# Larger weight loads, two columns through all weights first, columns 2 and 3 transposed by DMA: a gated unit beside a spectral filter

## The chip, the cores and the metric

The kernel runs on one core of a Trainium2 chip. The metric is the device time of one execution in microseconds (us), as a median of several executions. All traces shown are of executions in the fast state, with a granted TensorE clock of 0.998 or more. One execution of the kernel before was slow (183.37, clock 0.991); it counts in the median of its batch, 180.18 (180.00 without it), and not in the ratios. Ratios are the mean time of one kernel's fast runs over that of the other's in the same rounds, so they are not quite the ratio of the medians quoted beside them. An effect of 1 us is 0.56%. The medians of the kernel before lie up to 0.5% apart from batch to batch (179.32 to 180.18), so a kernel is compared only with the kernel before of its own batch.

## The reference, cut to what matters

```python
x  = A_x                                   # 2048 rows of 512, bf16
xn = layernorm(x)                          # over the 512
X  = rfft2(xn) * (w_r + 1j*w_i)            # spectral filter
A  = irfft2(X)
g  = xn @ w_gate;  u = xn @ w_up           # 512 -> 1792
B  = (gelu(g) * u) @ w_down                # 1792 -> 512
return x + A + B
```

The 2048 rows are held as 16 "columns" of 128 rows. The 1792 hidden features are 14 "weight columns" of 128. The gated unit is the large part of the matmul work; the spectral transform is done by matrix products in between.

## The kernel before: the parts that matter

The kernel makes its own plan: each operation has an engine, a guessed duration, dependencies and a priority, and a small planner puts them in an order per engine. In the traces each engine takes its instructions in that order; semaphores only make it wait.

```python
plan = _Plan({"S": 4, "G": 2, "U": 2, "ge": 3, ...})   # buffers: two PSUM banks for u
...
load_x(0, 1); d_ident = load_ct("ident", ...); load_x(1, 1)
load_w(0, 2, ("SP", "ACT")); load_x(2, 2); load_w(2, 4); load_w(4, 6)
load_x(4, 4); load_w(6, 10); load_x(8, 4); load_w(10, 14)
...
for c in range(4):                 # columns 0 to 3: transposed by TensorE
    ...; pe_transpose(c, -28 + 3 * c)
for c0, n, due in ((4, 2, 14), (6, 2, 16), (8, 4, 24), (12, 4, 32)):
    layernorm(c0, n, due)
    for c in range(c0, c0 + n): dma_transpose(c, due)
...
# glu(c0, n, f0, nf): n columns, nf weight columns: g_ps, u_ps on TensorE,
# ge = gelu(g_ps) on ScalarE, hT = u_ps * ge on VectorE, which frees the PSUM bank of u_ps
FIRST = [(0, 1, 0, 4), (1, 1, 0, 4), (0, 2, 4, 2), (2, 2, 0, 2), (2, 2, 2, 2), (2, 2, 4, 2)]
for c, n, f, nf in FIRST + [(0, 4, f, 1) for f in range(6, NFC)]: glu(c, n, f, nf)
```

The names in the traces: `x_t` input, `st` its statistics, `xn` normalized, `tp` transposes on TensorE, `xnT` transposed activations, `g_ps`/`u_ps` gate and up products, `hT` their product, `xf` a fold of `xn` for the transform, `bp` the first transform product, `RF_t` its table, `TW` the filter table, fetched by gathers on GpSimd. PE is TensorE, PEld its weight loads, DVE is VectorE, ACT ScalarE, POOL GpSimd; SPq and ACTq are the DMA issues of SyncE and ScalarE. PSUM is the memory that TensorE writes its products to.

## Time and profile before

| | before |
|---|---|
| time, median (first three runs) | 179.28 us |
| span of the trace | 177.6 us |
| first gated matmul | 6.89 us |
| end of the last product | 174.86 us |

Matmuls are pipelined, so the busy share hides small holes. I found gaps by the pitch: a group of n matmuls that starts at t is through its issue at t + n times the price of its width (0.056, 0.109, 0.2155 us for 128, 256, 512 columns), and the gap is what lies between that and the start of the next group.

### The profile page before, as it was taken

How to read it: one execution, taken by the hardware profiler on the slowest of the kernel's cores; microseconds unless marked ns; L12 is line 12 of the kernel's file. 1: busy time of each engine (PE TensorE's matmuls, PEld its weight loads, DVE VectorE, ACT ScalarE, POOL GpSimd, SP SyncE). 2: the span in 40 equal slices, each digit the busy share in tenths (PEclk: the TensorE clock that was granted, in tenths of full speed). 3: DMA queues.
4: the chain of work that ended last, by engine and by line, in shares of the span. 5: the costliest groups of instructions: out<-in, count | busy, mean ns of one | idle time of the engine just before them, and what ended most of it. 6: DMA issues, size and time to landing. Idle time of an engine off the chain costs nothing.

```text
span 177.6 us, 3041 instructions
## 1 busy us (share of the span) xinstructions
PE 173.4 (98%) x1100; PEld 92.9 (52%) x1100; DVE 118.1 (66%) x266; ACT 87.4 (49%) x158; POOL 18.6 (10%) x33
## 2 busy tenths in 40 slices
PE   6999999999999999999999999999999999999993
PEld 2598545545554544554555455554445444544463
DVE  1869999999537995889999885336442541632522
ACT  3162437456789737999998855453111211211100
POOL 3212138743200000000000000000000000000000
PEclk9999999999999999999999999999999999999999
DMA  5999487999297001302211121100222221322212
GB/s 144 311 355 359 86 270 84 223 296 193 52 347 255 2 0 29 93 2 59 61 48 37 37 59 37 27 0 0 84 68 66 83 89 59 92 80 69 74 45 59
DMA packets 23182, 19.24 MB, mean 108 GB/s; under 512 B 8512, under 2 KB 21824, under 8 KB 23168
## 3 DMA queue, kind: packets, MB, share of 16 engines
q1 hardware_dynamic: 22176, 17.57, 35.0%
q0 software_dynamic: 320, 1.19, 3.1%
q10 hardware_dynamic: 672, 0.30, 0.6%
q8 instruction: 8, 0.13, 0.3%
q14 instruction: 6, 0.05, 0.1%
HBM read 13.28 MB, written 2.10 MB: 87 GB/s over the span
## 4 chain that ended last, share of the span: by engine, by line
PE 91%; ACT 3%; DVE 3%; issue 1%; POOL 0%; DVEq 0%; POOLq 0%
PE u_ps L502 25%; PE g_ps L502 25%; PE warm L380 3%; ACT E L652 2%; PE yp L818 2%; PE bp L581 2%; PE gp L767 2%; PE yp__2078 L872 2%; PE yp__1994 L872 2%; PE yp__1967 L872 2%; PE yp__1936 L872 2%; PE yp__1909 L872 2%; PE yp__1820 L872 2%; PE yp__1793 L872 2%; PE yp__1762 L872 2%; PE yp__1735 L872 2%
## 5 line engine op out<-in xcount | busy, mean ns | idle before, releaser
L502 PE MATMUL g_ps<-xnT,Wg_sb 128*128 128x512 bf16 (+2 forms) x264 | 58.1, 347 | 0.0
L502 PE MATMUL u_ps<-xnT,Wu_sb 128*128 128x512 bf16 (+2 forms) x264 | 57.9, 347 | 0.0
L527 DVE TENSOR_TENSOR hT<-u_ps,ge 128x512 bf16<-128x512 f32 x56 | 38.4, 685 | 17.5 <-PE u_ps L502 14.4
L519 ACT ACTIVATE ge<-g_ps 128x512 bf16<-128x512 f32 x56 | 33.5, 598 | 30.5 <-PE g_ps L502 26.5
L502 PEld LDWEIGHTS <-Wu_sb 128*128 128x128 bf16 x264 | 24.3, 98 | 22.3 <-DMA Wu_sb<-in_B_w_up_dram 0.2
L502 PEld LDWEIGHTS <-Wg_sb 128*128 128x128 bf16 x264 | 24.3, 98 | 20.7 <-issue 0.2
L872 PEld LDWEIGHTS <-hT 128*128 128x128 bf16 x252 | 23.0, 98 | 21.9
L824 ACT CAST yf<-yp 128x512 bf16<-128x512 f32 x16 | 9.3, 586 | 37.6 <-PE yp L818 37.6
L652 ACT CAST E<-ep 64x512 bf16<-64x512 f32 x32 | 18.5, 579 | 1.1 <-PE ep L646 0.7
L396 DVE BATCH_NORM_STATS2 st<-x_t 128x6 f32<-128x512 bf16 x16 | 10.5, 676 | 4.8 <-DMA x_t<-in_A_x_dram 4.8
L629 ACT CAST ds<-dp 128x512 bf16<-128x512 f32 x16 | 8.8, 589 | 1.1 <-PE dp L624 1.0
L773 ACT CAST Gs<-gp 128x512 bf16<-128x512 f32 x16 | 8.6, 593 | 1.0 <-PE gp L767 1.0
L406 POOL TENSOR_TENSOR rstd<-ve,half 128x2 f32<-128x2 f32 (+2 forms) x7 | 6.6, 949 | 21.9 <-DVE ve L404 21.9
L585 ACT CAST Bs<-bp 128x512 bf16<-128x512 f32 x16 | 8.3, 603 | 0.5 <-PE bp L581 0.5
L818 PEld LDWEIGHTS <-Gs 128*128 128x128 bf16 x64 | 4.8, 98 | 3.5
L380 PE MATMUL warm<-warm 128*128 128x512 bf16 (+1 forms) x14 | 5.1, 539 | 1.3 <-POOL half L373 1.3
L412 DVE TENSOR_SCALAR xn<-x_t,mv,rstd 128x512 bf16<-128x512 bf16 (+1 forms) x17 | 6.1, 399 | 0.3 <-POOL rstd L406 0.3
L818 PE MATMUL yp<-CT,Gs 128*128 128x128 bf16 x64 | 6.0, 219 | 0.0
L683 DVE TENSOR_TENSOR m<-X,TW 128x1024 bf16<-128x1024 bf16 x8 | 5.5, 692 | 0.2
L624 PEld LDWEIGHTS <-Bs 128*128 128x128 bf16 x64 | 4.4, 98 | 2.4
L689 DVE TENSOR_TENSOR m<-X,TW 128x1024 bf16<-128x1024 bf16 x8 | 5.5, 684 | 0.0
L646 PE MATMUL ep<-ds,CT 128*128 128x512 bf16 x16 | 5.4, 379 | 0.0
(103 smaller groups left out, 169.0 us busy)
## 6 DMA issues: line engine op xcount, KB each, us to landing
y<-in_A_x_dram SPq DMA_DIRECT2D x16, 128.0 KB, 2.1
F<-F SPq DMA_DIRECT2D x32, 64.0 KB, 2.0
out_dram<-y SPq DMA_DIRECT2D x15, 128.0 KB, 1.7
Wd_sb<-in_B_w_down_dram SPq DMA_DIRECT2D x2, 896.0 KB, 8.3
x_t<-in_A_x_dram SPq DMA_DIRECT2D x3, 512.0 KB, 6.8
Wg_sb<-in_B_w_gate_dram SPq DMA_DIRECT2D x2, 512.0 KB, 6.8
Wu_sb<-in_B_w_up_dram SPq DMA_DIRECT2D x2, 512.0 KB, 9.1
Wg_sb<-in_B_w_gate_dram SPq DMA_DIRECT2D x3, 256.0 KB, 5.1
```

What stands on the lines that cost most here:

```text
L380: nc.tensor.matmul(tiles["warm"][:, 0:w], lhsT=warm[:, 0:P], rhs=warm[:, 0:w], start=True, stop=True)
L396: V.bn_stats(out=st[:], in_=x_t[:, c])
L502: nc.tensor.matmul(tiles[f"{nm}.{key}"][:, f * w:f * w + w], lhsT=W[:, e, (f0 + f) * P:(f0 + f + 1) * P], rhs=rhs(e), start=(f + e == 0), ...
L519: nc.scalar.activation(out=e[:, 0:nf * w], in_=tiles[f"g_ps.{key}"][:, 0:nf * w], func=AF.Gelu_apprx_tanh)
L527: V.tensor_tensor(out=out, in0=tiles[f"u_ps.{key}"][:, 0:nf * w].rearrange("p (f w) -> p f w", w=w) if nf > 1 else tiles[f"u_ps.{key}"][:, ...
L585: nc.scalar.copy(out=o, in_=tiles[f"bp.{cg}.{q}"][:].rearrange("p c (r g a) -> p (c r) g a", r=2, a=4))
L629: nc.scalar.copy(out=ds[:].rearrange("p (s k t) -> p s k t", s=2, t=2), in_=tiles[f"dp.{G}"][:].rearrange("p s t k -> p s k t"))
L652: nc.scalar.copy(out=tiles[f"E.{g}"][64 * h:64 * h + 64, r], in_=tiles[f"ep.{g}.{h}"][64 * r:64 * r + 64])
L773: nc.scalar.copy(out=o, in_=tiles[f"gp.{g}.{h}"][:].rearrange("p q (n a) -> p (q n) a", a=4))
L818: nc.tensor.matmul(yp[:, q], lhsT=tiles["G"][:, q, c], rhs=IQ[q], start=(q == 0), stop=(q == 3), skip_group_check=True)
L824: nc.scalar.copy(out=tiles[f"yf.{c // 2}"][:, c % 2], in_=tiles[f"yp.{c}"][:])
L872: nc.tensor.matmul(y[:, s], lhsT=tiles[sb, f][:, cl * P:(cl + 1) * P], rhs=Wd_sb[:, f, s], start=(f == 0), stop=False)
```

## The change

It is meant to start the gated product earlier and to keep it fed. The first two columns go through all weights before columns 2 and 3 are touched, so the latter can come later and be transposed by DMA rather than on TensorE.

```diff
-    load_w(0, 2, ("SP", "ACT")) ... load_x(2, 2) ... load_x(4, 4) ... load_x(8, 4) ...
+    d_g = [load_first(e, eng) for e, eng in ((0, "ACT"), (2, "SP"))]   # gate 0..3, 2 x 256 KB
+    d_u = load(..., Wu_sb[:, :, 0:4 * P], ...)                         # up 0..3, 512 KB
+    load_w(4, 8, (8.4, 10.9), lambda: load_x(2, 2, 9.6))               # columns 2, 3 in between
+    load_w(8, 12, ...); load_w(12, 14, ...)
@@ pe_transpose: one PSUM tile for each half of a column, not one for both
@@
-    for c in range(4): ... pe_transpose(c, -28 + 3 * c)
+    pe_transpose(0, -28); dummies(GAP, ...); pe_transpose(1, -25)      # GAP 4 -> 2
+    for c0, n, due in ((2, 2, -40), (4, 2, 14), (6, 2, 16), (8, 4, 24), (12, 4, 32)):
         layernorm(...)
         for c in range(c0, c0 + n): dma_transpose(c, due)
+        if c0 == 2:
+            load_x(4, 4, 0.0, deps=XN[3], prio=-80.0)
+            load_x(8, 4, 0.0, deps=XN[3], prio=-80.0)
+            d_rf = load(... RF_t ..., XN[3], prio=-80.0)
+            load_x(12, 4, 0.0, deps=XN[3], prio=-80.0)
@@ gathers of the filter table: after the last transposes (before: after column 11)
@@ first products: depth halves outermost, four weight columns per step
-    FIRST + [(0, 4, f, 1) for f in range(6, NFC)]
+    glu(0,1,0,4); glu(1,1,0,4); glu(0,2,f,2) for f in 4,6..12; glu(2,2,f,2) for f in 0,2..12
@@ w_down loaded by one DMA, not two; column 1 normalized in halves
@@ planner: given guessed landing times; no guessed hop between two operations of one engine
```

More of the change, by code (lines that the diff above doesn't have):

```diff
@@ L125 @@
 class _Op:
-    __slots__ = ("eng", "dur", "fn", "deps", "prio", "new", "use", "lag", "n", "start", "end", "kind", "nbytes")
+    __slots__ = ("eng", "dur", "fn", "deps", "prio", "new", "use", "lag", "n", "start", "end", "kind", "nbytes", "land")
 class _Plan:
@@ L135, in __init__, with op @@
         self.ops, self.bufs = [], dict(bufs)
-    def op(self, eng, dur, fn, deps=(), prio=0.0, new=(), use=(), lag=0.0, nbytes=0):
+    def op(self, eng, dur, fn, deps=(), prio=0.0, new=(), use=(), lag=0.0, nbytes=0, land=0.0):
         o = _Op()
+        o.land = land
         o.eng, o.dur, o.fn, o.prio, o.lag, o.nbytes = eng, dur, fn, prio, lag, nbytes
@@ L172, in run @@
                         continue
-                    at = max([d.end + d.lag + self.HOP for d in o.deps if d.eng != "PE" or o.eng != "PE"] + [0.0])
+                    at = max([d.end + (0.0 if d.eng == o.eng and not d.nbytes else d.lag + self.HOP)
+                              for d in o.deps if d.eng != "PE" or o.eng != "PE"] + [0.0])
                     if o.nbytes and o.eng != "POOL" and len(lanes) >= 8:
@@ L195, in run @@
                     wire = max(wire, o.end + 1.0) + o.nbytes / 0.34e6
-                    o.end = wire + 1.0
+                    o.end = o.land or wire + 1.0
                     if o.eng != "POOL":
@@ L311, with load_x, load_w @@
     o_eps = add("POOL", 0.15, lambda: nc.gpsimd.memset(eps[:], EPS), (), -30, lag=0.05)
-    def load_x(c0, n, eng="SP", deps=()):
+    def load_x(c0, n, land, eng="SP", deps=(), **kw):
         q = nc.sync if eng == "SP" else nc.scalar
-        o = load(n * P * D * 2, lambda: q.dma_start(out=x_t[:, c0:c0 + n], in_=x_v[:, c0:c0 + n]), deps, eng=eng)
+        o = load(2 * n * P * D, lambda: q.dma_start(out=x_t[:, c0:c0 + n], in_=x_v[:, c0:c0 + n]), deps, eng=eng, land=land, **kw)
         for c in range(c0, c0 + n):
             XD[c] = o
-    def load_w(f0, f1, engs=("SP", "SP")):
+    def load_w(f0, f1, lands, mid=lambda: None, deps=(), **kw):
         a, b = f0 * P, f1 * P
         os = []
-        for t, v, e in ((Wg_sb, wg_v, engs[0]), (Wu_sb, wu_v, engs[1])):
-            q = nc.sync if e == "SP" else nc.scalar
-            os.append(load(NE * P * P * 2 * (f1 - f0),
-                           lambda t=t, v=v, q=q: q.dma_start(out=t[:, :, a:b], in_=v[:, :, a:b]), eng=e))
+        for t, v, land in ((Wg_sb, wg_v, lands[0]), (Wu_sb, wu_v, lands[1])):
+            os.append(load(NE * P * P * (f1 - f0), lambda t=t, v=v: nc.sync.dma_start(out=t[:, :, a:b], in_=v[:, :, a:b]), deps, **kw,
+                           land=land))
+            if len(os) == 1:
+                mid()
         for f in range(f0, f1):
-            WD[f] = os
+            WD[f] = [[o] for o in os]
     def load_ct(first, last, eng="SP", deps=(), **kw):
@@ L332, in load_ct, with load_first @@
         return load(P * 2 * (b - a), lambda: q.dma_start(out=CT[:, a:b], in_=cap[:, a:b]), deps, eng=eng, **kw)
-    load_x(0, 1)
-    d_ident = load_ct("ident", "ident", "ACT")
-    load_x(1, 1)
-    load_w(0, 2, ("SP", "ACT"))
+    def load_first(e, eng):
+        q = nc.sync if eng == "SP" else nc.scalar
+        return load(P * P * 8, lambda: q.dma_start(out=Wg_sb[:, e:e + 2, 0:4 * P], in_=wg_v[:, e:e + 2, 0:4 * P]), eng=eng,
+                    land=5.1)
+    load_x(0, 1, 3.15)
+    d_ident = load_ct("ident", "ident", "ACT", land=2.9)
+    load_x(1, 1, 4.2)
+    d_g = [load_first(e, eng) for e, eng in ((0, "ACT"), (2, "SP"))]
     add("ACT", 1.3, lambda: nc.scalar.activation(out=eps[:, 1:2], in_=eps[:, 0:1], func=AF.Gelu_apprx_tanh),
         (o_eps,), -900)
-    load_x(2, 2)
-    load_w(2, 4)
-    load_w(4, 6)
-    load_x(4, 4)
-    load_w(6, 10)
-    load_x(8, 4)
-    load_w(10, 14)
+    d_u = load(NE * P * P * 4, lambda: nc.sync.dma_start(out=Wu_sb[:, :, 0:4 * P], in_=wu_v[:, :, 0:4 * P]), land=7.0)
+    for f in range(4):
+        WD[f] = [d_g, [d_u]]
+    load_w(4, 8, (8.4, 10.9), lambda: load_x(2, 2, 9.6))
+    load_w(8, 12, (12.2, 13.6))
+    load_w(12, 14, (14.3, 15.0))
     g_idx = add("POOL", 0.8, lambda: nc.gpsimd.dma_start(out=idx_t[:], in_=idx_d), (), -10, lag=3.0)
@@ L374 @@
     wb = _Buf("S")
-    NWARM, NGAP, GAP = 10, 1, 4
+    NWARM, NGAP, GAP = 10, 1, 2
     def warm_mm(w):
@@ L405, in layernorm, with normalize @@
             out=ve[:, k], in0=mv[:, k, 1], scalar1=EPS, scalar2=None, op0=ALU.add), ag, due - 5)
+        normalize(c0, n, due, e, halves)
+    def normalize(c0, n, due, e, halves, mean=None, op=ALU.subtract):
+        k = slice(c0, c0 + n)
         r = add("POOL", 0.55, lambda: nc.gpsimd.tensor_tensor(
@@ L412, in layernorm, with ev @@
                 XN[c].append(dve(0.04 + 0.29 / halves, lambda c=c, d=d: V.tensor_scalar(
-                    out=xn[:, c, d], in0=x_t[:, c, d], scalar1=mv[:, c, 0:1], scalar2=rstd[:, c:c + 1],
-                    op0=ALU.subtract, op1=ALU.mult), (r,), due - 2.5))
-        return ag
+                    out=xn[:, c, d], in0=x_t[:, c, d], scalar1=mv[:, c, 0:1] if mean is None else mean,
+                    scalar2=rstd[:, c:c + 1], op0=op, op1=ALU.mult), (r,), due - 2.5))
     def pe_transpose(c, due):
         XT[c] = []
-        b = _Buf("S")
         n = len(XN[c])
         for h in range(n):
+            b = _Buf("S")
             es = range(h * NE // n, (h + 1) * NE // n)
             def mm(h=h, es=es):
-                if h == 0:
-                    psum(f"tp.{c}", [P, NE, P], BF16)
+                psum(f"tp.{c}.{h}", [P, NE, P], BF16)
                 for e in es:
-                    nc.tensor.transpose(tiles[f"tp.{c}"][:, e], xn[:, c, e * P:(e + 1) * P], ident)
-            def ev(es=es, eng=(nc.scalar.copy, V.tensor_copy)[h]):
-                eng(out=xnT[c // 4][:, es[0]:es[-1] + 1, c % 4], in_=tiles[f"tp.{c}"][:, es[0]:es[-1] + 1])
-            o = pe(0.24 / n, mm, (XN[c][h], d_ident), due - 2, new=(b,) if h == 0 else (), use=(b,))
+                    nc.tensor.transpose(tiles[f"tp.{c}.{h}"][:, e], xn[:, c, e * P:(e + 1) * P], ident)
+            def ev(h=h, es=es, eng=(nc.scalar.copy, V.tensor_copy)[h]):
+                eng(out=xnT[c // 4][:, es[0]:es[-1] + 1, c % 4], in_=tiles[f"tp.{c}.{h}"][:, es[0]:es[-1] + 1])
+            o = pe(0.24 / n, mm, (XN[c][h], d_ident), due - 2, new=(b,))
             XT[c].append((act, dve)[h](0.1 + 0.35 / n, ev, (o,), due - 30, use=(b,)))
@@ L438, in dma_transpose @@
                     XN[c], due - 30, lag=1.0)]
-    first = layernorm(0, 1, -28, (), 2)
-    layernorm(1, 1, -25, first)
-    for c in range(4):
-        if c == 2:
-            layernorm(2, 2, -22, XT[0])
-        pe_transpose(c, -28 + 3 * c)
-        if c < NGAP:
-            dummies(GAP, -29.9 + 3 * c, XN[c], P)
-    for c0, n, due in ((4, 2, 14), (6, 2, 16), (8, 4, 24), (12, 4, 32)):
-        layernorm(c0, n, due)
+    layernorm(0, 1, -28, (), 2)
+    layernorm(1, 1, -25, (), 2)
+    pe_transpose(0, -28)
+    dummies(GAP, -29.9, XN[0], P)
+    pe_transpose(1, -25)
+    for c0, n, due in ((2, 2, -40), (4, 2, 14), (6, 2, 16), (8, 4, 24), (12, 4, 32)):
+        layernorm(c0, n, due, XN[max(c0 - 4, 1)])
         for c in range(c0, c0 + n):
             dma_transpose(c, due)
-        if c0 == 6:
+        if c0 == 2:
+            load_x(4, 4, 0.0, deps=XN[3], prio=-80.0)
+            load_x(8, 4, 0.0, deps=XN[3], prio=-80.0)
             d_rf = load(P * NC * P * 2, lambda: nc.sync.dma_start(
-                out=RF_t[:], in_=rf_d.rearrange("p (c k) -> p c k", c=NC)), XN[7])
-            load_x(12, 4, deps=XN[7])
+                out=RF_t[:], in_=rf_d.rearrange("p (c k) -> p c k", c=NC)), XN[3], prio=-80.0)
+            load_x(12, 4, 0.0, deps=XN[3], prio=-80.0)
     d_ct = load_ct("F0", "M0", deps=XN[11], prio=0.0)
@@ L463 @@
             d_tw.append(dma(P * n * 2, lambda k=k, c=c, s=s, a=a, n=n: gather(k, s, c, a, n),
-                            [g_idx] + XN[11], 20, eng="POOL", issue=1.2))
+                            [g_idx] + [o for t in range(12, NC) for o in XT[t]], 20, eng="POOL", issue=1.2))
     HT, hT_new = {}, {}
@@ L499, in mm @@
                 psum(f"{nm}.{key}", [P, D], tag=tag)
-            for f in range(a, b):
-                for e in range(NE):
-                    nc.tensor.matmul(tiles[f"{nm}.{key}"][:, f * w:f * w + w], lhsT=W[:, e, (f0 + f) * P:(f0 + f + 1) * P],
-                                     rhs=rhs(e), start=(f + e == 0), stop=(f == nf - 1 and e == NE - 1),
-                                     skip_group_check=nf > 1)
+            for f, e in sorted(((f, e) for f in range(a, b) for e in range(NE)), key=lambda k: (k[1] // 2, k)):
+                nc.tensor.matmul(tiles[f"{nm}.{key}"][:, f * w:f * w + w], lhsT=W[:, e, (f0 + f) * P:(f0 + f + 1) * P],
+                                 rhs=rhs(e), start=(f + e == 0), stop=(f == nf - 1 and e == NE - 1),
+                                 skip_group_check=nf > 1)
         g = [o for c in range(c0, c0 + n) for o in XT[c]]
-        step = min(nf, 2)
+        step = 4 if n == 1 else min(nf, 2)
         us = []
@@ L511, in glu @@
             new = [([], []), ([gb], [ub])][a == 0]
-            g = [pe(step * dur, lambda a=a: mm("g_ps", Wg_sb, "G", a, a + step), deps + [WD[f0 + a][0]], t,
+            g = [pe(step * dur, lambda a=a: mm("g_ps", Wg_sb, "G", a, a + step), deps + WD[f0 + a][0], t,
                     new=new[0], use=(gb,))]
-            us = [pe(step * dur, lambda a=a: mm("u_ps", Wu_sb, "U", a, a + step), us + g + [WD[f0 + a][1]], t,
+            us = [pe(step * dur, lambda a=a: mm("u_ps", Wu_sb, "U", a, a + step), us + g + WD[f0 + a][1], t,
                      new=new[1], use=(ub,))]
@@ L535, in glu @@
         return h
-    FIRST = [(0, 1, 0, 4), (1, 1, 0, 4), (0, 2, 4, 2), (2, 2, 0, 2), (2, 2, 2, 2), (2, 2, 4, 2)]
-    for c, n, f, nf in FIRST + [(0, 4, f, 1) for f in range(6, NFC)]:
-        glu(c, n, f, nf)
+    for c in range(2):
+        glu(c, 1, 0, 4)
+    for f in range(4, NFC, 2):
+        glu(0, 2, f, 2)
+    for f in range(0, NFC, 2):
+        glu(2, 2, f, 2)
     FOLD, PS_, DS_, CS_, FI_, IC_ = {}, {}, {}, {}, {}, {}
@@ L802 @@
     d_ri = dma(P * NC * P * 2, load_ri, [PS_[3, q] for q in range(4)], 70)
-    d_wd = [dma(P * 7 * D * 2, lambda k=k: nc.sync.dma_start(
-        out=Wd_sb[:, 7 * k:7 * k + 7], in_=wd_v[:, 7 * k:7 * k + 7]), [PS_[3, q] for q in range(4)], 71 + k)
-        for k in range(2)]
+    d_wd = [dma(P * (b - a) * D * 2, lambda a=a, b=b: nc.sync.dma_start(
+        out=Wd_sb[:, a:b], in_=wd_v[:, a:b]), [PS_[3, q] for q in range(4)], 71 + a)
+        for a, b in ((0, 14),)]
     yfb, lvb = {}, {}
```

## The prediction

> **What bounds the kernel now.** I read the page's busy shares first, then the chain of work that ended last in order of time, then the timeline of the first twenty microseconds. The busy shares and the head of the chain:
>
> ```profile
> PE 173.4 (98%) x1100; PEld 92.9 (52%) x1100; DVE 118.1 (66%) x266; ACT 87.4 (49%) x158; POOL 18.6 (10%) x33
> ...
> PE 91%; ACT 3%; DVE 3%; issue 1%; POOL 0%; DVEq 0%; POOLq 0%
> ```
>
> TensorE is busy 98% of a span of 177.6 us, and 91% of the chain that ended last is TensorE's own work. So the time is: the moment the first useful matmul starts, plus the matmul work, plus gaps, plus the tail after the last matmul. The chain in order of time (start, us, what) gives the first term and the price of each kind of matmul:
>
> ```profile
> 1.34 4.44 PE warm L380 x10
> 5.79 0.64 PE tp L428 x4
> 6.43 0.43 PE warm L380 x4
> 6.89 0.82 PE g_ps L502 x8
> 7.72 0.45 PE u_ps L502 x8
> 8.16 0.22 PE tp L428 x4
> ...
> 8.84 0.62 PE u_ps L502 x8
> 9.46 0.45 PE g_ps L502 x8
> ...
> 11.25 0.45 PE tp L428 x8
> 11.70 0.87 PE g_ps L502 x8
> ...
> 18.68 0.86 PE g_ps L502 x4
> ```
>
> The gated product starts at 6.89 us and from 9.46 on one group follows the other. Prices: eight 128-wide matmuls 0.45 us (0.056 each), eight 256-wide 0.87 (0.109), four 512-wide 0.86 (0.2155). A check that this is really the bound: the groups by shape count 641 matmuls of 512 columns, 79 of 256 and, after the first four transposes and the warm-up, 362 of 128. 641 x 0.2155 + 79 x 0.109 + 362 x 0.056 = 138.1 + 8.6 + 20.3 = 167.0 us. From 6.89 to the end of the last product (174.08 + 0.78) are 167.97 us. All gaps together are therefore about 1.0 us. Two of them are in the lines above: the first group of eight took 0.82 in place of 0.45 (0.37 lost), and the group at 8.84 took 0.62 (0.17 lost). About 0.4 us is spread over the rest.
>
> The timeline (start, us, engine, what, idle before and its releaser) names both:
>
> ```profile
> 6.47 0.37 ACT L431 COPY xnT<-tp 128x256 bf16<-128x256 bf16 x1 [3.29 <-PE tp L428]
> 6.88 0.29 DVE L431 COPY xnT<-tp 128x256 bf16<-128x256 bf16 x1 [0.83 <-ACT xnT L431]
> 6.90 0.65 PEld L502 LDWEIGHTS <-Wg_sb 128*128 128x128 bf16 x7 [0.20 <-issue]
> 8.84 0.45 PEld L502 LDWEIGHTS <-Wu_sb 128*128 128x128 bf16 x8 [0.18 <-DMA Wu_sb<-in_B_w_up_dram]
> ```
>
> The transposed first column is evicted in two halves from one PSUM tile. ScalarE's half starts only when all four transposes are through (5.79 + 0.64 = 6.43), and VectorE's half starts 0.04 us after ScalarE's ends, at 6.88, although VectorE had been idle 0.83 us. The first matmul needs the first half, the third needs the second half, which is there at 6.88 + 0.29 = 7.17: this is the 0.37. The 0.17 is the second pair of up weights landing late.
>
> **What the Trainium skill says.** "TensorE: Matmul & The Clock Gate", section "Wait — 56ns, not 53.3ns?", gives a warm matmul as columns over 2.4 GHz plus about 2.5 ns: 55.6 and 215.7 ns for 128 and 512 columns. The trace agrees (0.056 and 0.2155), and its 256-wide groups give 0.109. So cutting a 512-wide matmul in two costs about 2.5 ns. The same page, Part 1, says the array runs at half rate until about 3.4 us of sustained work. The trace agrees: ten 512-wide warm-up matmuls took 4.44 us, 0.44 each, twice the later price, and the four dummies at 6.43 took 0.107 each; from 7.72 on all is at full rate. "DMA: Bandwidth & Descriptors", section "Specifications", gives about 358 GB/s as one core's share of HBM; the page's slices 3 and 4 show 355 and 359 GB/s. The same page, "Issuing engines are not separate DMA queues", says that a load issued from ScalarE uses the same 16 engines and saves only issue time. So spreading the first gate weights over two issuers cannot make the bytes arrive at a higher rate. That one no view of this run separates.
>
> **The change part by part.**
> 1. Each half of a first-column transpose gets its own PSUM tile. The first pair of transposes is through about 0.33 us before the second (half of the chain's 0.64), so ScalarE's copy can begin near 6.13 in place of 6.47 and end near 6.50; VectorE's no longer follows ScalarE and ends near 6.75. The gated product starts near 6.55, 0.34 earlier.
> 2. Matmuls of a single column run all four weight columns over the first half of the depth, then over the second. The second half is first needed by the ninth matmul, so the 0.37 stall goes. Against this, the start now lies before the clock opens, which I put at 7.0 (the g group at 6.89 still has about one slow matmul, the u group none): about four matmuls at 0.107 rather than 0.056 lose 0.2. Sum of 1 and 2: before, sixteen matmuls were through at 8.16; after, 6.55 + 4 x 0.107 + 12 x 0.056 = 7.65. Gain 0.5 us.
> 3. Columns 2 and 3 are transposed by DMA: eight TensorE transposes go, 0.45 us at 11.25 on the path. Gain 0.45. ScalarE loses two copies of 0.59, off the path.
> 4. Weight columns 6 to 13 of the first four activations are done in two halves of two columns: 64 matmuls of 512 (13.8 us) become 128 of 256 (13.95). Loss 0.15 to 0.2. The number of activations and products is the same: 14 groups before (3 + 3 + 8) and after (2 + 5 + 7), 512 wide each.
> 5. Weights come in larger pieces: 512 KB of gate, then 512 KB of up. The wait of 0.17 at 8.84 goes. But up weights are now first needed near 7.65, and before them lie 128 + 32 + 128 + 512 + 512 = 1,312 KB. Before, 1,568 KB were in by 8.84. At 311 to 355 GB/s (slices 2 and 3) the 256 KB less are 0.75 to 0.85 us: landing near 8.0. A wait of 0.35 is likely, less if the longer rows stream better. I count 0.25. Later needs: gate 4 to 7 near 10.5, 512 KB after, 9.5; up 4 to 7 near 11.4 with 768 KB more, 11.5; the next at 13.0 and 14.5 against needs of 14.0 and 14.9. Close, with 0.1 us or so to lose.
> 6. The warm dummies after the first transposes drop from four to two. They stood in a wait; nothing changes but the room for the earlier start.
> 7. Later inputs (columns 4 to 15 and the transform table) load after columns 2 and 3 are normalized, the gathers move behind the last normalization, and the down weights come in one piece. All off TensorE's path if nothing runs dry.
>
> Sum: 0.5 + 0.45 + 0.17 - 0.18 - 0.25 = 0.69, or about 0.7 us: 179.28 - 0.7 = 178.6.
>
> **The rivals.** First, **the DMA transposes come late**. Columns 2 and 3 would land near 10, be normalized near 13.3 (two statistics at 0.68, POOL 0.9, two normalizations at 0.4 with products between) and the transposes, median 3.4 us to landing and behind up to 1 MB of weights, be there by 17 to 18. The need comes when five groups of 1.75 us are done, near 19.3. For: only 1.5 us of room. Against: the twelve transposes of before all stay under 5.3 us. If it fails, up to 1 to 2 us are lost, 180.
>
> Second, **the transform path becomes the end**. VectorE is full from 16 to 40 us, ScalarE 18.9 of 20 us at 80 to 100, and their last product into TensorE (gp at 114.71) lies only 5 us ahead of the end of the gated products. Had VectorE stood idle from 13 to 18 waiting for columns 4 to 7, that would be eaten. Against: the fold of columns 0 to 3, 2.7 us, can fill that hole, and its table now comes before 22 us. The gathers, six of 0.95 to 1.7 us and 4.9 to land, start after 38 rather than at 27, so the table fix would end near 53 to 55; its first reader on VectorE was at 55.6. Tight. A slip of 3 us is absorbed, more is paid one for one: 180 to 181.
>
> Third, **the head gains but the weights take it back**: the product is then at the weights' delivery rate until 15 us, and the gain of point 2 becomes waits. Then only points 3 and 4 remain, 0.3 us: 179.0.
>
> Fourth, **everything lands as planned** and no wait takes the place of the old one: 178.2.
>
> **Range and chances.** No term is near 3.6 us, which 2% would be; only 1.0 us of gaps and 5.8 us of start are there to take, and the start hangs on the landing of the first column (statistics at 3.51), which stays. So faster by 2% needs something I don't see. Slower by 2% needs both first rivals at their worst. I take 178.5, between the sum and the fourth rival, and 177.5 to 179.9 for the range, wider upward because of the first two; faster 0.02, same 0.95, slower 0.03.
>
> **What would show it.** The first gated matmul near 6.55 and VectorE's half copied before ScalarE's ends (1); eight matmuls without a hole before the second half, some at 0.107 (2); no eight transposes near 11 (3); 96 matmuls of 256 columns each for gate and up (4); a weight-load wait on the up weights near 7.7 under 0.4 (5). I am wrong if TensorE shows a gap near 19 before columns 2 and 3, if the gap sits before the inverse products near 115 to 120, or if the clock opens a whole window later, which would cost 1.7 us.

## The result, and the profile after

The changed kernel takes 180.51 us (179.99 to 180.72, six runs) against 179.45 (179.19 to 180.03): a ratio of 1.0050, 95% interval 1.0028 to 1.0071. It is about 1 us **slower**, still within 2%; the prediction was 0.7 us of gain, with a range up to 179.9.

First the chain in order of time (start, us, what):

```profile
5.79 0.30 PE tp L436 x2
6.12 0.38 ACT xnT L439
6.54 1.05 PE g_ps L508 x16
7.59 0.22 PE tp L436 x4
...
10.49 0.87 PE g_ps L508 x8
...
20.97 0.89 PE g_ps L508 x8
21.86 0.66 DVE st L402
22.52 0.60 DVE hT L533
23.17 1.03 PE u_ps L508 x8
```

The head is what was hoped for. The product starts at 6.54, sixteen matmuls are through at 7.59 (8.16 before), and the first 256-wide group starts at 10.49; before it started at 11.70. The lead is 1.21 us. Then, near 21.86, the chain leaves TensorE for VectorE: statistics and a product of VectorE stand in TensorE's way.

The timeline shows what stands there (start, us, engine, what, and in brackets the idle time before it with its releaser):

```profile
7.91 2.00 SPq L325 DMA_DIRECT2D Wu_sb<-in_B_w_up_dram  x1
12.75 2.39 SPq L445 DMA_TRANSPOSE xnT<-xn  x1
15.24 1.21 SPq L445 DMA_TRANSPOSE xnT<-xn  x1
16.50 1.05 SPq L317 DMA_DIRECT2D x_t<-in_A_x_dram  x2
18.19 1.04 PE L508 MATMUL u_ps<-xnT,Wu_sb 128*128 128x256 bf16 x8
21.04 0.69 DVE L402 BATCH_NORM_STATS2 st<-x_t 128x6 f32<-128x512 bf16 x1 [2.76 <-DMA x_t<-in_A_x_dram]
21.86 0.66 DVE L402 BATCH_NORM_STATS2 st<-x_t 128x6 f32<-128x512 bf16 x1
22.44 0.67 DVE L533 TENSOR_TENSOR hT<-u_ps,ge 128x512 bf16<-128x512 f32 x1
23.17 1.03 PE L508 MATMUL u_ps<-xnT,Wu_sb 128*128 128x256 bf16 x8 [1.32 <-DVE hT L533]
```

Read it from the end. The up product at 23.17 waited for a product `hT` of VectorE, because that frees one of the two PSUM banks. The `hT` at 22.44 belongs to the up product of 18.19, which was done near 19.2. It came three microseconds late because VectorE's order has the statistics of columns 4 and 5 ahead of it, and those waited 2.76 us for input. The input was there only at 21.04 because its load went out only at 16.50. SyncE had two transposes to issue first: its last weight load was issued at 9.91 (7.91 + 2.00), then it stood until 12.75, since a transpose needs a normalized column (the normalization of columns 2 and 3 started at 12.31), and the transposes kept it until 16.45. The load itself waits for no normalization at run time; only the plan put it behind (moved ahead, it goes out at 10.00, below).

The windows of four microseconds (busy time of each engine with the instructions in parentheses, then granted clock, DMA share, GB/s) tell the same; first before, then after:

```profile
16.00:20.00 4.00, 4.00 (x32) 2.94 (x31) 4.00 (x12) 1.61 (x3) 1.63 (x2) 1.00 0.72 205
20.00:24.00 4.00, 4.00 (x20) 1.84 (x19) 4.00 (x12) 1.38 (x3) 0.14 (x1) 1.00 0.49 97
```

```profile
16.00:20.00 4.00, 4.00 (x39) 3.57 (x37) 1.94 (x4) 1.20 (x2) 0.00 (x0) 1.00 0.64 165
20.00:24.00 4.00, 2.68 (x25) 2.26 (x24) 2.90 (x8) 1.20 (x2) 0.52 (x1) 1.00 0.96 390
```

The third figure after the window's length is VectorE: full before, 1.94 and 2.90 of 4.00 us after. The first is TensorE: 2.68 of 4.00 in the second window after. VectorE has the same work to do later, and this shows near 48 us:

```profile
43.52 1.65 DVE L422 TENSOR_SCALAR xn<-x_t,mv,rstd 128x512 bf16<-128x512 bf16 x4 [0.30 <-POOL rstd L416]
47.62 0.69 DVE L576 TENSOR_TENSOR xf<-A 128x1024 bf16<-128x1024 bf16 x1
48.37 0.84 PE L590 MATMUL bp<-RF_t,xf 128*128 128x128 bf16 x12 [0.43 <-DVE xf L576]
```

The transform product `bp` had to stop in the middle until VectorE's last fold was done at 48.31.

By pitch the gaps of the changed kernel are 1.48 us near 22, 0.59 near 48 and 0.27 near 85 (the last was there before, 0.28 near 75). **The account closes**: lead of 1.21 us at the first 256-wide group, less 2.07 for the two new gaps, less 0.16 for 64 wide matmuls cut in two (128 x 0.109 - 64 x 0.2155), leaves TensorE 1.02 us behind (of these two traces, one execution each). Its last product ends at 175.94 in place of 174.86, 1.08 behind. After 120 us both kernels run without a difference: 54.72 us remain before and 55.84 after, and the 1.12 more are 20 transform products of 128 columns (0.056 each) that had still to be done there.

### The profile page after: what moved, and what is told of

It reads as the page before. It is cut to its first block, busy times and chain, and to the rows that moved or that the text cites. A ratio compares the mean times of both kernels' runs of the same rounds, so it can differ in the third digit from the quotient of the medians.

```text
span 178.7 us, 3152 instructions
## 1 busy us (share of the span) xinstructions
PE 172.4 (96%) x1154; PEld 98.2 (55%) x1154; DVE 119.6 (67%) x268; ACT 86.0 (48%) x156; POOL 16.0 (9%) x33
## 3 DMA queue, kind: packets, MB, share of 16 engines
q0 software_dynamic: 320, 1.19, 2.4%
## 4 chain that ended last, share of the span: by engine, by line
PE 85%; DVE 9%; DMA 2%; issue 1%; ACT 1%; DVEq 0%
PE u_ps L508 24%; PE g_ps L508 23%; DVE hT L533 3%; PE yp L827 2%; PE bp L590 2%; PE gp L776 2%; PE yp__2132 L881 2%; PE yp__2106 L881 2%; PE yp__2079 L881 2%; PE yp__2048 L881 2%; PE yp__2021 L881 2%; PE yp__1932 L881 2%; PE yp__1905 L881 2%; PE yp__1873 L881 2%; PE yp__1845 L881 2%; PE yp__1700 L881 2%
## 5 line engine op out<-in xcount | busy, mean ns | idle before, releaser
L508 PEld LDWEIGHTS <-Wu_sb 128*128 128x128 bf16 x296 | 27.3, 98 | 20.3 <-issue 1.7
L508 PEld LDWEIGHTS <-Wg_sb 128*128 128x128 bf16 x296 | 27.3, 98 | 18.9 <-issue 0.2
L416 POOL TENSOR_TENSOR rstd<-ve,half 128x2 f32<-128x2 f32 (+2 forms) x7 | 6.0, 858 | 35.4 <-DVE ve L410 35.4
L849 DVE TENSOR_TENSOR lv<-yf 128x512 bf16<-128x512 bf16 x8 | 3.4, 423 | 7.8 <-ACT yf L833 7.1
L386 PE MATMUL warm<-warm 128*128 128x512 bf16 (+1 forms) x12 | 4.4, 534 | 1.3 <-POOL half L379 1.3
L827 PE MATMUL yp<-CT,Gs 128*128 128x128 bf16 x64 | 5.5, 219 | 0.0
```

The lines of the kernel that those rows point to most:

```text
L508: nc.tensor.matmul(tiles[f"{nm}.{key}"][:, f * w:f * w + w], lhsT=W[:, e, (f0 + f) * P:(f0 + f + 1) * P], rhs=rhs(e), start=(f + e == 0), ...
L827: nc.tensor.matmul(yp[:, q], lhsT=tiles["G"][:, q, c], rhs=IQ[q], start=(q == 0), stop=(q == 3), skip_group_check=True)
```

## The experiments

Most of them edit the finished order of the changed kernel, not its priorities, since a changed dependency lets the planner move hundreds of instructions. The edit is then one or a few moved instructions. Three runs were planned anew: c1, a3 and v1. In the traces of a3 and v1 some 300 of 1,154 matmuls and 100 of 268 instructions of VectorE stand elsewhere than in the changed kernel. A summary first (us, medians; ratio to the kernel before of the same batch):

| run | edit | median | before | ratio (95%) | gaps of TensorE in its trace |
|---|---|---|---|---|---|
| changed, first result | none | 180.51 | 179.45 | 1.0050 (1.0028 to 1.0071) | 1.48 at 22, 0.59 at 48 |
| z_after_third | none | 180.28 | 179.32 | 1.0054 (1.0038 to 1.0070) | 0.85 at 22, 0.58 at 48 |
| z_after_again | none | 181.06 | 180.18 | 1.0029 (0.9978 to 1.0081) | 1.25 at 22, 0.59 at 48, 0.8 at 52 |
| a1_x47_first | load of columns 4 to 7 ahead of the transposes | 178.79 | 179.46 | 0.9973 (0.9960 to 0.9985) | 0.44 at 11 |
| a1_again | the same | 179.08 | 179.32 | 0.9980 (0.9961 to 0.9999) | 0.42 at 19, 0.64 at 23 |
| a2_products_first | two products ahead of the statistics | 180.66 | 179.46 | 1.0070 (1.0057 to 1.0083) | 0.64 at 23, four of 0.15 to 0.25, 0.59 at 48 |
| a3_gathers_back | gathers as before | 179.46 | 179.46 | 1.0010 (0.9997 to 1.0023) | 0.84 at 22 |
| a4_x47_scalar | that load from ScalarE | 179.84 | 180.18 | 0.9967 (0.9920 to 1.0014) | 0.14 at 23, 1.0 at 50 |
| c1_pe_transposes | columns 2, 3 on TensorE, planned anew | 182.90 | 180.18 | 1.0154 (1.0100 to 1.0209) | 1.5 from 30 to 35, 2.15 at 50 |
| c2_pe_same_order | columns 2, 3 on TensorE, order kept | 179.16 | 179.32 | 0.9991 (0.9970 to 1.0012) | 0.65 at 11, 1.07 at 15 |
| v1_x47_gathers | a1 and a3 together | 179.80 | 180.18 | 0.9952 (0.9903 to 1.0002) | 0.76 at 15, 0.92 at 41, 0.37 at 48 |
| v5_table_second | a1, and the table ahead of columns 8 to 11 | 179.82 | 180.15 | 0.9972 (0.9927 to 1.0017) | 0.56 at 7, 1.1 at 50 |
| b2_two_tiles_halves | the kernel before with parts 1 and 2 alone | 179.34 | 179.46 | 0.9994 (0.9981 to 1.0007) | 0.31 and 0.41 before 9.3 |

All were correct. A trace is one execution; where two of the same kernel are shown, the gaps differ by several tenths of a microsecond. The batch of z_after_again, a4, c1 and v1 ran on a noisier chip (the kernel before 179.59 to 183.37, the slow execution included), as did v5's.

**The load moved (a1_x47_first, a1_again).** One instruction of SyncE goes ahead of two others:

```diff
     order = plan.run()
+    ahead(XD[4], XT[2][0])   # load of columns 4 to 7 before the transpose of column 2
```

> The changed kernel with one instruction moved: the load of columns 4 to 7 is issued on SyncE ahead of the two DMA transposes of columns 2 and 3 instead of behind them. The order on TensorE, VectorE, ScalarE and GpSimd is the same, line for line. Theory (held queue): in the changed kernel SyncE spends 12.75 to 16.45 us on those two transposes, so the load goes out at 16.50 and lands at 21.04; VectorE stands 2.76 us before its first statistics, the products queued behind it come late, and TensorE loses about 1.5 us near 22 and 0.6 near 48. So here VectorE's wait on the input falls under 0.5 us, both gaps go, and the time is 178.3 to 178.8 us, 1.0 to 1.2% under the changed kernel and 0.3 to 0.6% under the kernel before. Rival A (the transform path is the bound because the table fix is planned late): the two gaps close but the time comes back later, 180.0 us or more. Rival B (the transposes themselves come late behind the extra 512 KB): a gap near 19 us before the products of columns 2 and 3, 179.5 us or more.

> The load of columns 4 to 7 ahead of the transposes, once more, beside the unaltered changed kernel on the same chip. 0.995 to 0.998 of the kernel before; no gap near 22 or 48 us. If the first result was luck, it lies at 1.000 or above.

Its trace, the same views:

```profile
10.00 1.34 SPq L317 DMA_DIRECT2D x_t<-in_A_x_dram  x1
12.78 3.34 SPq L445 DMA_TRANSPOSE xnT<-xn  x2
18.23 0.69 DVE L402 BATCH_NORM_STATS2 st<-x_t 128x6 f32<-128x512 bf16 x1
```

The load goes out at 10.00 and the statistics start at 18.23 with no wait named. Both gaps are gone, and the time falls to 178.79, 0.27% under the kernel before and 0.8% under the changed kernel: inside the expected time, a little less than the expected shares. The second run gives 0.998, beside 1.0054 for the unaltered kernel on the same chip. So both new gaps hang on where this one load stands. The move spares the load SyncE's wait for the normalization and the issue of the transposes alike; no run separates the two. In the second trace the moved bytes do cost something: 0.42 us at 19 before columns 2 and 3 (TensorE waited for a transpose), which is rival B of the expectation in small, and 0.64 at 23 for the transform table, where no gap near 22 was expected.

**The order of VectorE alone (a2_products_first).** The load stays late; the statistics of columns 4 to 6 are put behind the two products.

```diff
+    held = [...]                       # statistics that hang on the load of columns 4 to 7
+    order[b:b] = held                  # b: just behind the product of columns 2, 3, weights 0, 1
```

> The changed kernel with only VectorE's order altered: the two products that stand behind the statistics of columns 4 to 6 come ahead of them. The load of columns 4 to 7 still goes out at 16.5 us and lands at 21. Theory (held queue): the gap of 1.3 to 1.5 us on TensorE near 22 us goes although the bytes come just as late; the smaller gap near 48, VectorE's backlog, stays in part. Time 179.0 to 179.4 us. If instead the late bytes cost through VectorE's backlog alone, the gap near 48 grows by what the gap near 22 shrinks, and the time stays at 180.2 to 180.6.

```profile
19.60 0.69 DVE L534 TENSOR_TENSOR hT<-u_ps,ge 128x512 bf16<-128x512 f32 x1 [1.05 <-PE u_ps L509]
21.35 0.69 DVE L534 TENSOR_TENSOR hT<-u_ps,ge 128x512 bf16<-128x512 f32 x1 [1.05 <-PE u_ps L509]
21.95 0.69 DVE L402 BATCH_NORM_STATS2 st<-x_t 128x6 f32<-128x512 bf16 x1
23.47 1.05 PE L592 MATMUL bp<-RF_t,xf 128*128 128x128 bf16 x16 [0.48 <-DMA RF_t<-spec_rf]
```

The products come in time, and no up product waits for them near 22. Yet my 179.0 to 179.4 was wrong: the time stayed at 180.66. TensorE now waits at 23.47 for the transform table, which also stands behind the transposes in SyncE's order, and then several times for VectorE. Its gaps from 22 us on add up to about 2.0 us, as in the changed kernel (2.07). The other theory of the expectation had the time about right (up to 180.6), but not the way: the gap near 48 did not grow, it stayed at 0.59. So the held products were only the first of several waits on the same late loads. Mending an order downstream of a late load moved the wait here; it didn't remove it.

**Who holds the load (a4_x47_scalar).** The same load is issued by ScalarE, near 11.4 us, and SyncE issues its transposes as in the changed kernel.

```diff
+            XD[4].fn = lambda: nc.scalar.dma_start(out=x_t[:, 4:8], in_=x_v[:, 4:8])
+    ahead(XD[4], XT[2][0])
```

> The changed kernel with the load of columns 4 to 7 issued from ScalarE after its third activation, near 12 us, while SyncE issues the two transposes at the same time as before. This tells apart what holds the load. Theory (SyncE's order holds it: the transposes keep the issuer busy, the DMA engines have room, 0.25 to 0.56 of them busy at 16 to 18 us): the load lands by 17.5, VectorE waits under 0.7 us, the gap near 22 is gone, 178.5 to 179.1 us. Rival (the DMA engines themselves are held by the transposes and the last weights): the load lands at 19.5 or later whoever issues it, the gap stays over 0.7 us, 179.6 us or more.

```profile
11.40 0.35 ACTq L459 DMA_DIRECT2D x_t<-in_A_x_dram  x1
12.83 3.59 SPq L445 DMA_TRANSPOSE xnT<-xn  x2
18.29 0.69 DVE L402 BATCH_NORM_STATS2 st<-x_t 128x6 f32<-128x512 bf16 x1
```

SyncE is as busy as ever, and still the statistics start at 18.29, with no wait named and 2.75 us earlier than in the changed kernel. So the DMA engines were able to carry the load; it was the place in SyncE's queue that held it. The time is less clear: 179.84 misses the expected 178.5 to 179.1 and lies in the rival's range, on a chip where the kernel before took 180.18. The ratio of 0.9967 lies where that of a1 does, though the interval is wide and reaches past 1, and another gap of 1.0 us, near 50, is in this trace (below). The waits decide between the two theories, not the time.

**Undoing the DMA transposes (c1_pe_transposes, c2_pe_same_order).** In the first try the planner ordered anew:

```diff
-            dma_transpose(c, due)
+            (pe_transpose if c0 == 2 else dma_transpose)(c, 14 if c0 == 2 else due)
```

> The changed kernel with one part undone: columns 2 and 3 are transposed by TensorE again, the rest of the change stays (the planner orders anew). With no transpose in SyncE's way the later loads go out right behind the weights, near 10 us. The prediction's term: eight transposes more on TensorE's path, 0.45 us. Theory: no gap near 22, and 0.45 us more work than the kernel with the load moved ahead (178.8), so 179.0 to 179.5 us, under the changed kernel by 1 us although it does more work. Rival (the DMA transposes are not what costs): 180.6 to 181.0, the 0.45 on top of the changed kernel.

It took 182.90, far from both theories. The gap at 22 is gone, but the new order has 1.5 us of gaps from 30 to 35 and one of 2.15 at 50. This run says nothing of the transposes, only that a new plan is a new kernel. The second try puts the eight transposes and two ScalarE copies into the old order near 16 us and leaves all else where it was:

```diff
+    for c in (2, 3):
+        XT[c][0].fn = by_pe(c)            # four transposes, one ScalarE copy
+        order.remove(XT[c][0])
+        order.insert(order.index(HOP_[0, 2, 8]), XT[c][0])
```

> Columns 2 and 3 transposed by TensorE again, this time with no new planning: the eight transposes and two ScalarE copies are put into the changed kernel's own order near 16 us, every other instruction stays where it is (an earlier try let the planner reorder, which brought other waits). The two DMA transposes no longer stand ahead of the later loads, so those go out near 10 us. Theory: no wait near 22, and the eight transposes cost 0.45 us on TensorE, so 0.4 to 0.5 us above the kernel with the load moved ahead: 0.998 to 1.001 of the kernel before. If the DMA transposes were free of side effects, it would lie 0.45 us above the changed kernel, at 1.006 to 1.009.

It takes 179.16 (0.9991), 1.1 us less than the changed kernel beside it, **although TensorE does 0.45 us more**. That is what the held queue says. The difference to a1 on the same chip is 0.08 us in the medians and 0.11% in the ratios, less than the 0.45 us of the transposes, and the intervals overlap. So a1's gain over c2 isn't settled. Its trace is of its slowest execution (span 178.9), with up weights landing late at 11 and 15, and I take no term from it.

**The gathers (a3_gathers_back, v1_x47_gathers).**

```diff
-   [g_idx] + [o for t in range(12, NC) for o in XT[t]], 20, eng="POOL"
+   [g_idx] + XN[11], 20, eng="POOL"
```

> The changed kernel with one part undone: the six gathers of the filter table again stand behind the third group of columns instead of behind the last transposes. The planner then puts the filter's first multiplication on VectorE earlier (69.9 us in the changed kernel, 55.6 before). Theory (held queue near 21 us): this part costs nothing, since after 120 us the changed kernel shows no more gap than before; the time stays 180.2 to 180.8. Rival A (the transform path, started 14 us late, is what costs): the time falls by 0.7 us or more, to 179.8 or less, with the gap near 22 us still there.

The ratio fell from 1.0050 to 1.0010, the time to 179.46, so my "costs nothing" was wrong, and the rival's number came true. But the traces don't show the rival's reason. In the changed kernel the filter's first multiplication stands at 69.87 on VectorE, 14 us later than before, and this cost nothing that a trace shows: after 120 us the gaps are the same. What is gone from this trace is the gap near 48, 0.59 of about 0.7 us. With the gathers ahead of the last normalization on GpSimd, the planner put two fold steps ahead of that normalization on VectorE:

```profile
43.54 0.69 DVE L572 TENSOR_TENSOR xf<-A 128x1024 bf16<-128x1024 bf16 x1
44.75 1.37 DVE L422 TENSOR_SCALAR xn<-x_t,mv,rstd 128x512 bf16<-128x512 bf16 x4
46.64 0.68 DVE L576 TENSOR_TENSOR xf<-A 128x1024 bf16<-128x1024 bf16 x1
47.13 1.09 PE L590 MATMUL bp<-RF_t,xf 128*128 128x128 bf16 x16
```

The last fold starts at 46.64 rather than 47.62 and `bp` doesn't stop. Its gap near 22 is still there (0.84). So the gap near 48 seems to have two parents: VectorE's lost time, which a1 gives back with the order unchanged (shown), and the order of normalization and fold, which a3 changes among much else (read from its trace, not isolated). In its trace either repair closes the gap.

> Both repairs in one: the load of columns 4 to 7 ahead of the transposes, and the gathers back behind the third group of columns. The gap near 48 us that the gathers' place was worth is already gone with the load moved, so the two gains do not add: 178.4 to 178.9 us, within 0.3 us of the load moved alone (178.79). If they add, 177.7 to 178.1.

Both together took 179.80, outside both expectations, on the noisy chip; the ratio is 0.9952 with an interval of 0.9903 to 1.0002. That neither shows nor excludes that the gains add. Its own trace has other gaps (up weights at 15, 0.92 at 41), and after the one at 41 `bp` stops again for VectorE's last fold, 0.37 us at 48, so the order of a3 doesn't close that gap in every execution.

**The head alone (b2_two_tiles_halves).** The first two parts of the change in the kernel before; the plan's order stays, and within a group the matmuls take the depth in halves. It is part 2 in small: a group still has two weight columns (four in the change), and column 1 is normalized in one piece:

```diff
-                if h == 0:
-                    psum(f"tp.{c}", [P, NE, P], BF16)
+                psum(f"tp.{c}.{h}", [P, NE, P], BF16)
...
-            for f in range(a, b):
-                for e in range(NE):
+            for f, e in sorted(((f, e) for f ... for e ...), key=lambda k: (k[1] // 2, k)):
```

> The kernel before with the first two parts of the change alone: one PSUM tile for each half of a transpose, and the depth taken in halves by the first products. The order of instructions on every engine is that of before. As the prediction counted it, the first gated matmul comes near 6.55 in place of 6.89, the hole of 0.37 us goes, and the time falls by 0.5 us to 178.9. Rival (the head is tied to the weights): the start moves to 6.55 just the same, but the second pair of up weights still lands at 8.8, TensorE waits for it 0.5 us or more in place of 0.17, and the time stays within 0.15 us of before, 179.3 to 179.6.

```profile
6.93 0.61 PE L501 MATMUL g_ps<-xnT,Wg_sb 128*128 128x128 bf16 x8
9.24 0.45 PEld L501 LDWEIGHTS <-Wu_sb 128*128 128x128 bf16 x8 [0.43 <-DMA Wu_sb<-in_B_w_up_dram]
```

In this execution the first transposes came at 6.19, 0.40 later than in the trace of before, so times are best counted from there. The first product starts 0.74 us after them (1.10 before), without the hole. But the second pair of up weights is awaited until 9.24, 3.05 us after the transposes, and 8.84 - 5.79 = 3.05 before as well. In these two traces the head's gain is given back to the weights to the hundredth; the time is 0.9994 of before. The rival is right: under the old order of the weight loads parts 1 and 2 are worth nothing measurable. That the new order makes them pay is argued from the lead of 1.21 us; no run has the new order without them.

**Controls and a last try (z_after_again, z_after_third, v5_table_second).**

> The changed kernel again, unaltered, as the control of this batch and for a second trace. 180.0 to 180.7 us. If the gap near 22 us is the rule and not one execution's, it is here again, 1.2 to 1.6 us, and the load of columns 4 to 7 lands 4 us or more after its issue at about 16.5.

> The changed kernel unaltered, as the control of this batch, since the last batch ran on a noisier chip. 1.003 to 1.007 of the kernel before, with the gap near 22 us again 1.2 to 1.6 us.

The loss of the changed kernel is steady (1.0050, 1.0029, 1.0054), and so is the late load: issue at 16.50 and 16.29, statistics at 21.05 and 20.79. The size of the first gap is not steady: 0.85 in the third trace, where 1.2 to 1.6 was expected. There TensorE had lost 0.27 and 0.16 us before it, waiting for up weights, and the statistics began 0.25 us earlier; the end of the gap is tied to them. The time of z_after_again, 181.06, is above the expected 180.7, as the kernel before was slower on that chip.

> A try at a version that beats both: the load of columns 4 to 7 ahead of the transposes, and behind them the transform table ahead of columns 8 to 11 (in one trace of the moved load TensorE waited 0.64 us near 23 for that table, in another it did not wait). No wait for the table; 0.994 to 0.998 of the kernel before, that is the same as the load moved alone or up to 0.3 us less. If columns 8 to 11 now come too late, VectorE waits for them near 24 us and the gain is gone, 0.999 or more.

```diff
+    ahead(XD[4], XT[2][0])
+    ahead(d_rf, XD[8])       # transform table before columns 8 to 11
```

No wait for the table was left, and the ratio is 0.9972, but the interval reaches from 0.9927 to 1.0017: not told apart from a1. The version that beats both kernels is a1.

**What stays open.** In the traces of a4, c1 and v5 TensorE loses 1 to 2.15 us near 50 us because `bp` waits for an eviction by ScalarE, while ScalarE stands idle over 2 us with a finished product before it. The trace names no releaser that fits. It isn't a matter of these variants alone: the unaltered changed kernel shows it in its second trace (z_after_again, 0.8 us at 52, ScalarE idle 0.86), and v1's 0.92 at 41 is a wait for ScalarE too, idle 2.57 us before it. The changed kernel's other two traces and a1's two don't show it. I have no cause for it.

## Why the prediction was wrong, by its own steps

- **Parts 1 and 2, the earlier start: right in the sum, by luck in two of its terms.** Start 6.54 (6.55 predicted), ScalarE's copy at 6.12 (6.13), sixteen matmuls through at 7.59 (7.65). But the four slow matmuls, 0.2 us, did not come: in the timeline the sixteen start at 6.54 and the next group at 7.43, 0.056 each from the first. And the hole before was 0.21, not 0.37: its eight matmuls start at 6.89 and the next group at 7.55, 0.66 for 0.45. (The chain's 0.82 and 1.05 have about 0.16 of a matmul's passage in them, as every first group after a wait.) The two errors cancel. The 3.4 us of work that the prediction quotes is not in its lines either: the dummies at 6.43 were still at half rate, 5.1 us after the warm-up's start. And b2 shows that the gain is not theirs alone.
- **Part 3, eight transposes off TensorE: right in the trace**, where columns 2 and 3 cost nothing at 11. The prediction missed what they do elsewhere: each holds SyncE, 2.39 and 1.21 us.
- **Part 4, 64 matmuls cut in two: right.** 96 matmuls of 256 columns for gate and for up, 0.109 us each.
- **Part 5, a new wait of 0.25 us on the up weights: not seen** in the first trace (the product started at 7.65, when it was ready), 0.27 and 0.16 us in the third. By the first 256-wide group the lead was 1.21 us where these terms gave 0.5 + 0.45 + 0.17 - 0.25 = 0.87.
- **Part 7 failed**: "All off TensorE's path if nothing runs dry." VectorE ran dry, 2.76 us, because the load of columns 4 to 7 stood in SyncE's order behind the transposes and what they wait for, and in an order that holds products for TensorE behind the dry instruction. The sum had no term for it; it measured 1.48 us near 22 and 0.59 near 48, together more than the whole predicted gain. That the load's place is the cause is shown by a1, twice, with one instruction moved.
- **The second rival named the hole and dismissed it.** The fold did fill 13.5 to 16.6 as it said. But the landing of columns 4 to 7 was taken as 18, without the time SyncE needs to issue two transposes ahead of the load, and came at 21.04. And the damage was looked for at the end of the transform path, near 115 to 120, where nothing happened; it came through the two PSUM banks of the up product, at once, and with that order mended (a2) through other waits soon after.
- **The first rival**, late transposes, did not occur in the changed kernel: columns 2 and 3 start on time at 19.07. It occurs in small (0.42 us) in one trace of a1, where 512 KB go ahead of them.

With the load repaired, the kernel takes 178.79 and 179.08 in two batches, 0.4 us on average under the kernel before. The rest of the predicted 0.7 is not accounted for gap by gap, since it changes from one execution to the next.

## What to carry to other kernels

A DMA issue is an instruction in the order of its engine: before a load is placed behind others, add up how long those hold the issuer and what they wait for, not only the bytes. When an engine's order is fixed, an instruction that waits for a late load holds everything behind it, so ask of each late load what stands behind its first reader and whose buffer that frees. A gain at the head counts only up to the next thing tied to the loads, and a test of one part alone shows whether it is worth anything by itself.

## What the Trainium skill lacked or had wrong

- "DMA: Bandwidth & Descriptors", section "Issuing engines are not separate DMA queues", says that issuing from several engines saves only the sequencer's time to initiate a DMA, "which is usually small relative to the DMA itself". It counts only that time. Here what stood ahead of the load in its issuer's order decided: behind two transposes and their wait it went out at 16.50, and its first reader started at 21.04; issued from ScalarE at 11.40, the reader started at 18.29.
- The same page, section "DMA Transpose (X-bar)", doesn't say how long one transpose of 128 x 512 holds the engine that issues it (cycle counts elsewhere on the page are for other shapes). In the changed kernel's trace the fourteen took 1.19 to 2.39 us, median 1.22, two of them over 2 us; why those two is not shown.
- No page that I used accounts for ScalarE standing 0.9 to 3.3 us, near 41 to 52, with its operand finished (0.86 us in z_after_again, 3.28 us in c1).
